# Splitting the first load of a decode attention kernel, and issuing it ahead of the branch into the block

## The chip, the core and the metric

The kernel runs on one core of one Trainium2 chip. The core has five engines with instruction streams of their own: TensorE (PE), VectorE (DVE), ScalarE (ACT), GpSimd (POOL) and SyncE (SP), which wait for each other on semaphores. Data come from HBM over 16 DMA engines, into an on-chip memory of 128 rows (partitions). The metric is the device time in microseconds; lower is better.

## The reference

One query position (Sq = 1) of 32 heads attends to 65,536 keys; four query heads share one of 8 key/value heads. All is bf16, D = 128. K and V have 134 MB each.

```python
B, Hq, Hkv, Sq, Sk, D = 1, 32, 8, 1, 65536, 128
k = jnp.repeat(k, rep, axis=1)          # rep = Hq // Hkv = 4
v = jnp.repeat(v, rep, axis=1)
scores = jnp.einsum("bhqd,bhkd->bhqk", q, k) * D ** -0.5
p = softmax(scores, axis=-1)
return jnp.einsum("bhqk,bhkd->bhqd", p, v)
```

## The kernel before

The keys of one head are cut into four units of 16,384 keys, and two units make a pair. There are 16 pairs, one for each lap of TensorE's loop. A pair's K is one transfer of 128 rows by 64 KB: row p holds 256 consecutive keys, 32 KB of them for the first unit (`n = 0`) and 32 KB for the second (`n = 1`). V is laid out in the same way. The buffers are `kbuf` and `vbuf` (both units), and `bbuf`, which holds the second unit's K so that `kbuf` can be loaded again early; in most laps POOL and ACT copy it from `kbuf`, in the others it comes straight from HBM.

For each unit TensorE transposes 128 tiles of 128 keys in groups of eight (`trb`, line 135), DVE and ACT copy the groups to `ktb` (lines 207 and 205), and TensorE multiplies them with the head's four queries (`qkb`, line 144). DVE takes the maximum, POOL reduces it over the rows, ACT makes the exponentials (`pts`, line 347), and TensorE multiplies those with V (`pvb`, line 162). After its last unit a head's sum is divided, and the result goes out at the end of the program.

All K and V transfers are issued by SP in program order (`sync_engine`, lines 398 to 448). K of lap p waits for `kfree` and V for `vfree`, which say that the buffer has been read. Lap 0 waits for nothing: its K comes in four pieces of 2 MB (`K_PIECES`, lines 26 and 407: two for `kbuf`, two for `bbuf`, each 128 rows by 16 KB), and then V as one transfer (line 437). Each piece has its own semaphore; `kp[0][0]`, here also called kp0_0, belongs to the first, and line 130 takes 16 from it ahead of a lap's first transposes. The last lap's V comes in pieces that get smaller (73, 38, 13 and 4 tiles, `V_PIECES`), so that the last piece to land is short. The 32 output rows are stored by SP at the end (lines 445 and 448).

In front of the loop DVE makes an identity matrix (`ident`), TensorE runs `PE_LEAD` small products whose result is not used (line 184), waits for the queries (`q_sem`), and transposes them. ACT issues the queries' load (line 372). Every engine enters its function by a branch into the block (lines 450 to 455), behind a barrier that all engines pass at the start of the program.

Of the kernel before, what the change touches and what calls it, by code (L numbers as in the profile page):

```python
# [10 lines left out]
P = 128  # L11
T = 128
# [4 lines left out]
LAG = 3  # L17


PE_LEAD = 48  # L20
CB = 16
HU = 4
Q = 32


K_PIECES = ((64, 64), (64, 64))
# [15 lines left out]
def starts(sizes):  # L42
    return [sum(sizes[:i]) for i in range(len(sizes))]
# [8 lines left out]
def bass_standalone__gqa_softmax__decode_kernel(nc, q, k, v, out):  # L52
    _, Hq, _, D = q.shape
# [4 lines left out]
    NP = NU // 2  # L58
    assert HR == Q and all(sum(x) == HR - R for x in OUT_ROWS) and D == P and Sk == P * T * HU and T * R == 512 and H >= 3 and HU == 4
    scale = float(D) ** -0.5  # L60
    kf, vf, qf, of = k[0], v[0], q[0, :, 0, :], out[0, :, 0, :]
# [4 lines left out]
    def sb(name, shape, dt):  # L66
        return S(nc.sbuf_tensor(name, shape, dt))

    def sem(name):
        return S(nc.semaphore(name))  # L70

    kbuf = sb("kbuf", [P, 2 * T * D], DT.bfloat16)
# [4 lines left out]
    qsb = sb("qsb", [HR, D], DT.bfloat16)  # L77
# [4 lines left out]
    identf = sb("identf", [P, P], DT.float32)  # L82
    ramp = sb("ramp", [P, Q], DT.float32)
    rampT = sb("rampT", [P, Q], DT.float32)
    cmax = sb("cmax", [P, R], DT.float32)
# [22 lines left out]
    kp = [[sem(f"kp{i}_{p}") for p in range(len(K_PIECES[i]))] for i in range(2)]  # L108
# [7 lines left out]
    cm, cma, ng, dmr, exd, sx, lrd, lra = (sem(n) for n in ("cm", "cma", "ng", "dmr", "exd", "sx", "lrd", "lra"))  # L116
    acr, l_sem, lws = sem("acr"), sem("l_sem"), sem("lws")
    xd, xa, xg = sem("xd"), sem("xa"), sem("xg")
    q_sem, o_sem, s_x, t_if, t_id, t_o, t_f, t_row = (
        sem(n) for n in ("q_sem", "o_sem", "s_x", "t_if", "t_id", "t_o", "t_f", "t_row"))  # L120

    def own(e, ins, s):
        ins.then_inc(s, 1)
        take(e, s)
# [43 lines left out]
    def pe_pair(pe, lap):  # L168
        pend = []
        for n in range(2):  # L170
            for j in range(G):
                pe_transposes(pe, n, j)
                pend.append((n, j))
                if len(pend) > LAG:
                    pe_scores(pe, *pend.pop(0))
        while pend:
            pe_scores(pe, *pend.pop(0))
        for n in range(2):
            pe_values(pe, n, lap)

    def tensor_engine(pe):
        pe.wait_ge(t_id, 1)
        for _ in range(PE_LEAD):
            pe.matmul(pvb[0][0:R, 0:R], lhsT=ident[:, 0:R], rhs=ident[:, 0:R], start=True, stop=True)
        pe.wait_ge(q_sem, 16)
        pe.transpose(qps[:, 0:HR], qsb[:, :], ident[0:HR, 0:HR]).then_inc(s_x, 1)
        pe.wait_ge(t_if, 1)
        with pe.Fori(0, NP) as lap:
            pe_pair(pe, lap)
        pe.wait_ge(t_f, H)  # L190
        pe.transpose(trb[0][0:R, 0:P], oT[:, HR - R:HR], ident[:, :]).then_inc(s_x, 1)  # L191
# [121 lines left out]
    def make_identity(e):  # L313
# [5 lines left out]
        w = 4  # L319
        while w < Q:  # L320
            own(e, e.tensor_scalar(ramp[:, w:2 * w], ramp[:, 0:w], float(w), None, ALU.add), xd)
            w *= 2
        own(e, e.transpose(rampT[:, :], ramp[:, :]), xd)
        for b in range(0, P, Q):
            ins = e.tensor_tensor(ident[b:b + Q, b:b + Q], ramp[b:b + Q, :], rampT[b:b + Q, :], ALU.is_equal)
        ins.then_inc(t_id, 1)
# [26 lines left out]
    def act_pair(e, lap):  # L353

        def copy(o, i):
            return e.activation(o, i, AF.Copy)  # L356

        for j in (3, 7, 11, 15):
            evict(e, 0, j)
            if j in ACT_COPIES:  # L360
                copy_unit(e, (lap - (WHOLE[0] - 1)) * (WHOLE[1] - lap) > 0, ACT_COPIES[j], copy, cpa, xa)
                if j == max(ACT_COPIES):
                    e.sem_inc(kfree, 1)
        for j in (3, 7):
            evict(e, 1, j)
        exps(e, 0)
        for j in (11, 15):
            evict(e, 1, j)
        exps(e, 1)

    def scalar_engine(e):
        e.dma_start(qsb[:, :], qf).then_inc(q_sem, 16)
        e.wait_ge(t_id, 1)
        e.activation(dscr[:, 0:1], ident[:, 0:1], AF.Exp, scale=1.0)
        e.activation(identf[:, :], ident[:, :], AF.Copy).then_inc(t_if, 1)
        with e.Fori(0, NP) as lap:
            act_pair(e, lap)
# [20 lines left out]
    def sync_engine(e):  # L398
        W = T * D

        def src(x, p):
            h, c = p // 2, p % 2
            return x[h, c * 2 * P * T:(c + 1) * 2 * P * T, :].rearrange("(p t) d -> p (t d)", p=P)

        def pieces(to, s, sizes, sems):
            for a, w, sm in zip(starts(sizes), sizes, sems):
                e.dma_start(to[:, a * D:(a + w) * D], s[:, a * D:(a + w) * D]).then_inc(sm, 16)

        def tokens(sems):
            for sm in sems:  # L410
                e.sem_inc(sm, 16)

        for p in range(NP):
            ks, vs = src(kf, p), src(vf, p)
            if p:
                e.wait_ge(kfree, 3 * p)
            if WHOLE[0] <= p < WHOLE[1]:
                e.dma_start(kbuf[:, :], ks).then_inc(kp[0][0], 16)
                tokens(kp[0][1:])
            else:  # L420
                for n in range(2):
                    if n and p:
                        e.wait_ge(bfree, p)
                    to, s = bbuf if n else kbuf, ks[:, n * W:(n + 1) * W]
                    if p == 0 or (p == NP - 1 and n == 0):
                        pieces(to, s, K_PIECES[n], kp[n])
                    else:
                        e.dma_start(to[:, 0:W], s).then_inc(kp[n][0], 16)
                        tokens(kp[n][1:])
                e.sem_inc(cpg, len(POOL_COPIES))  # L430
                e.sem_inc(cpa, len(sum(ACT_COPIES.values(), ())))
            if p:
                e.wait_ge(vfree, p)
            if WHOLE[0] <= p < WHOLE[1]:
                tokens(kp[1])
            if p < NP - 1:
                e.dma_start(vbuf[:, :], vs).then_inc(vp[0][0], 16)
                tokens(vp[1])
            else:
                for n in range(2):  # L440
                    pieces(vbuf[:, n * W:(n + 1) * W], vs[:, n * W:(n + 1) * W], V_PIECES[n], vp[n])
        e.wait_ge(t_o, H)
        for b, rows in enumerate(OUT_ROWS):
            for r, n in zip(starts(rows), rows):
                e.dma_start(of[r:r + n, b * Q:(b + 1) * Q],
                            orow[b * Q + r:b * Q + r + n, :]).then_inc(o_sem, 16)
        e.wait_ge(t_row, 1)
        e.dma_start(of[HR - R:HR, :], lrow[:, :]).then_inc(l_sem, 16)

    with nc.Block() as block:  # L450
        block.tensor(tensor_engine)
        block.vector(vector_engine)
        block.scalar(scalar_engine)
        block.gpsimd(gpsimd_engine)
        block.sync(sync_engine)
# [30 lines left out]
```

## Time and profile before

| What | Value |
|---|---|
| Median of 3 runs | 628.12 us (628.09 to 628.2) |
| Span of the profiled execution, first to last instruction | 626.9 us |
| Median less that span | 1.2 us |
| Read from HBM | 268.44 MB, 428 GB/s over the span |
| TensorE busy | 484.6 us (77%) |
| VectorE busy | 315.1 us (50%) |
| ScalarE busy | 228.9 us (37%) |
| GpSimd busy | 159.9 us (26%) |
| First K transfer issued | 0.72 us |
| First transposes of K | 8.18 us |

The times in the profile are counted from the first instruction's start. The span is the profiled execution's own time; the median is of other executions and includes what lies around the instructions. A line such as `L407 SPq DMA_DIRECT2D` is the time in which SP issues a transfer, not the transfer itself. In the stretches (a row begins with its start and end) the columns are the length, the busy time of TensorE's products, its weight loads, DVE, ACT and POOL with the number of instructions, TensorE's granted clock, the share of the 16 DMA engines, and GB/s; a transfer's bytes and time are counted in the stretch in which they start, so that a short stretch can show a share over 1.

### The profile page before, as it was taken

How to read it: one execution, taken by the hardware profiler on the slowest of the kernel's cores; microseconds unless marked ns; L12 is line 12 of the kernel's file. 1: busy time of each engine (PE TensorE's matmuls, PEld its weight loads, DVE VectorE, ACT ScalarE, POOL GpSimd, SP SyncE). 2: the span in 40 equal slices, each digit the busy share in tenths (PEclk: the TensorE clock that was granted, in tenths of full speed). 3: DMA queues.
4: the chain of work that ended last, by engine and by line, in shares of the span. 5: the costliest groups of instructions: out<-in, count | busy, mean ns of one | idle time of the engine just before them, and what ended most of it. 6: DMA issues, size and time to landing. Idle time of an engine off the chain costs nothing. (4 is left out here: it accounts for less than half of the span.)

```text
span 626.9 us, 27931 instructions
## 1 busy us (share of the span) xinstructions
PE 484.6 (77%) x12340; PEld 478.9 (76%) x12340; DVE 315.1 (50%) x699; ACT 228.9 (37%) x445; POOL 159.9 (26%) x124
## 2 busy tenths in 40 slices
PE   5752995959859498694976959679496894999698
PEld 5752995949859498694976959679496894999698
DVE  4620752817537174371734717356183562848274
ACT  2320532615335153341634407245062441624133
POOL 0000704307042070520605115060150702400000
PEclk9965875958769587695966959678596785969597
DMA  8999999999999999999999999999999999999997
GB/s 366 440 449 424 439 431 439 431 439 426 443 422 447 410 460 410 460 406 460 410 439 431 426 443 426 443 426 439 431 439 431 439 431 435 416 447 424 420 433 302
DMA packets 6280, 268.57 MB, mean 428 GB/s; under 512 B 896, under 2 KB 1024, under 8 KB 1152
## 3 DMA queue, kind: packets, MB, share of 16 engines
q1 hardware_dynamic: 6224, 268.45, 99.2%
q8 instruction: 6, 0.10, 0.1%
q10 hardware_dynamic: 48, 0.01, 0.0%
q14 instruction: 2, 0.02, 0.0%
HBM read 268.44 MB, written 0.01 MB: 428 GB/s over the span
## 5 line engine op out<-in xcount | busy, mean ns | idle before, releaser
L207 DVE COPY ktb<-trb 128x1024 bf16<-128x1024 bf16 x384 | 254.6, 689 | 177.5 <-PE trb L135 173.7
L205 ACT ACTIVATE ktb<-trb 128x1024 bf16<-128x1024 bf16 x128 | 131.0, 1023 | 352.7 <-PE trb L135 297.9
L135 PE MATMUL trb<-ident,kbuf 128*128 128x128 bf16 x2048 | 177.1, 245 | 104.7 <-PEq L49 104.6
L135 PEld LDWEIGHTS trb<-ident,kbuf 128*128 128x128 bf16 x2048 | 143.9, 111 | 105.6 <-issue 105.5
L213 POOL COPY bbuf<-kbuf 128x2048 bf16<-128x2048 bf16 x78 | 143.9, 1893 | 177.6 <-POOLq L49 177.6
L144 PE MATMUL qkb<-qcur,ktb 128*128 128x4 bf16 x4096 | 174.3, 165 | 11.8 <-PEq L49 10.3
L144 PEld LDWEIGHTS qkb<-qcur,ktb 128*128 128x128 bf16 x4096 | 155.2, 97 | 14.6 <-issue 14.6
L135 PE MATMUL trb<-ident,bbuf 128*128 128x128 bf16 x2048 | 157.0, 220 | 5.2 <-issue 3.9
L162 PE MATMUL pvb<-pts,vbuf 128*128 128x4 bf16 x4096 | 113.0, 166 | 15.2 <-PEq L49 11.0
L162 PEld LDWEIGHTS pvb<-pts,vbuf 128*128 128x128 bf16 x4096 | 111.1, 103 | 16.6 <-issue 15.6
L135 PEld LDWEIGHTS trb<-ident,bbuf 128*128 128x128 bf16 x2048 | 117.4, 97 | 5.5 <-issue 5.5
L393 POOL PARTITION_ALL_REDUCE cmaxa<-cmax x32 | 11.9, 370 | 254.1 <-POOLq L49 254.1
L347 ACT ACTIVATE pts<-qkb,negm 128x128 bf16<-128x128 f32 x128 | 50.9, 549 | 37.2 <-ACTq L49 37.2
L356 ACT ACTIVATE bbuf<-kbuf 128x2048 bf16<-128x2048 bf16 x26 | 49.5, 1902 | 0.0
L347 ACT ACTIVATION_READ_ACCUMULATOR pts<-qkb,negm 128x1 f32 x128 | 35.6, 278 | 0.0
L225 DVE TENSOR_REDUCE cmax<-qkb 128x4 f32<-128x512 f32 x32 | 22.0, 686 | 23.4 <-DVEq L49 23.4
L259 DVE TENSOR_TENSOR acc<-acc,pvb 128x4 f32<-128x4 f32 x16 | 2.5, 158 | 30.0 <-PE pvb L162 30.0
L257 DVE COPY acc<-pvb 128x4 f32<-128x4 f32 x8 | 1.3, 163 | 21.8 <-PE pvb L162 21.8
L395 POOL PARTITION_ALL_REDUCE la<-lp x8 | 3.4, 430 | 30.7 <-POOLq L49 30.7
L236 DVE SCALAR_TENSOR_TENSOR negm<-cmaxa,m 128x4 f32<-128x4 f32 x24 | 3.9, 163 | 11.7 <-DVEq L49 11.5
L351 ACT ACTIVATE alpha<-dm 128x4 f32<-128x4 f32 x32 | 7.1, 221 | 0.0
L250 DVE TENSOR_TENSOR acc<-acc,alpha 128x4 f32<-128x4 f32 x24 | 3.9, 164 | 6.1 <-DVEq L49 5.7
(44 smaller groups left out, 41.6 us busy)
## 6 DMA issues: line engine op xcount, KB each, us to landing
kbuf<-in_k_dram SPq DMA_DIRECT2D x4, 2048.0 KB, 16.3
bbuf<-in_k_dram SPq DMA_DIRECT2D x2, 4096.0 KB, 20.9
bbuf<-in_k_dram SPq DMA_DIRECT2D x2, 2048.0 KB, 19.9
kbuf<-in_k_dram SPq DMA_DIRECT2D x1, 4096.0 KB, 16.3
vbuf<-in_v_dram SPq DMA_DIRECT2D x1, 4096.0 KB, 21.9
vbuf<-in_v_dram SPq DMA_DIRECT2D x1, 2336.0 KB, 27.1
vbuf<-in_v_dram SPq DMA_DIRECT2D x1, 1216.0 KB, 29.6
vbuf<-in_v_dram SPq DMA_DIRECT2D x1, 416.0 KB, 30.1
```

The lines of the kernel that those rows point to most:

```text
L135: ins = pe.transpose(trb[j % NTB][:, i * P:(i + 1) * P], kv[:, t, :], ident[:, :])
L144: ins = pe.matmul(qkb[n][:, t * R:(t + 1) * R], lhsT=ktb[:, off:off + P], rhs=qcur[:, :], start=True, stop=True)
L162: ins = pe.matmul(pvb[n][:, 0:R], lhsT=vv[:, t, :], rhs=pts[n][:, t * R:(t + 1) * R], start=t == 0, stop=t == T - 1)
L205: e.activation(dst, trb[j % NTB][:, :], AF.Copy).then_inc(eva, 1)
L207: e.tensor_copy(dst, trb[j % NTB][:, :]).then_inc(evd, 1)
L213: ins = op(bbuf[:, c * CB * D:(c + 1) * CB * D], kbuf[:, off:off + CB * D])
L225: e.tensor_reduce(cmax[:, :], qkb[n][:, :].rearrange("p (t g) -> p g t", g=R), AX.X, ALU.max).then_inc(cm, 1)
L236: return e.scalar_tensor_tensor(to[:, :], cmaxa[:, :], -scale, mo[:, :], ALU.mult, ALU.min)
L347: ins = e.activation(pv[:, g, :], sv[:, g, :], AF.Exp, bias=negm[:, g:g + 1], scale=scale, accum_out=rsum[:, g:g + 1])
L351: e.activation(alpha[:, :], dm[:, :], AF.Exp, scale=1.0).then_inc(sx, 1)
L356: return e.activation(o, i, AF.Copy)
L393: e.partition_all_reduce(cmaxa[:, :], cmax[:, :], P, bass.bass_isa.ReduceOp.max).then_inc(cma, 1)
```

## The change

The first of lap 0's four K pieces is cut by rows. A load of its rows 0 to 15 (16 rows by 16 KB, `FIRST = 16`) is issued by SP from the main program, ahead of the branch into the block, on a new semaphore `kf0`. The other 112 rows follow as the first transfer in the block, on the semaphore that the whole piece had. ACT's load of the queries is moved ahead of the branch in the same way. TensorE waits for `kf0` once, ahead of its loop, and runs 47 warm-up products instead of 48. The other three K pieces and V of lap 0, and every later lap, are issued as before.

```diff
-PE_LEAD = 48
+PE_LEAD = 47
...
+FIRST = 16
...
+    kf0 = sem("kf0")
...
         pe.wait_ge(t_if, 1)
+        pe.wait_ge(kf0, 16)
         with pe.Fori(0, NP) as lap:
             pe_pair(pe, lap)
...
     def scalar_engine(e):
-        e.dma_start(qsb[:, :], qf).then_inc(q_sem, 16)
         e.wait_ge(t_id, 1)
...
-                    if p == 0 or (p == NP - 1 and n == 0):
+                    if p == 0 and n == 0:
+                        w = K_PIECES[0][0] * D
+                        e.dma_start(to[FIRST:P, 0:w], s[FIRST:P, 0:w]).then_inc(kp[0][0], 16)
+                        pieces(to[:, w:W], s[:, w:W], K_PIECES[0][1:], kp[0][1:])
+                    elif p == 0 or (p == NP - 1 and n == 0):
                         pieces(to, s, K_PIECES[n], kp[n])
...
+    w = K_PIECES[0][0] * D
+    nc.sync.dma_start(kbuf[0:FIRST, 0:w],
+                      kf[0, 0:2 * P * T, :].rearrange("(p t) d -> p (t d)", p=P)[0:FIRST, 0:w]).then_inc(kf0, 16)
+    nc.scalar.dma_start(qsb[:, :], qf).then_inc(q_sem, 16)
     with nc.Block() as block:
```

SP's instructions at the start of the program, before the change (a name in brackets is what the row waits for; sizes are rows by elements):

```order
L455 UNCONDITIONAL_BRANCH [waits barrier_Pool_Activation_PE_DVE_SP_release]
L407 DMA kbuf<-in_k_dram 128x8192 x2
L407 DMA bbuf<-in_k_dram 128x8192 x2
L437 DMA vbuf<-in_v_dram 128x32768
L418 DMA kbuf<-in_k_dram 128x32768 [waits kfree]
```

The same place on SP with the change:

```order
L457 DMA kbuf<-in_k_dram 16x8192 [waits barrier_Pool_Activation_PE_DVE_SP_release]
L465 UNCONDITIONAL_BRANCH
L429 DMA kbuf<-in_k_dram 112x8192
L409 DMA kbuf<-in_k_dram 128x8192
L409 DMA bbuf<-in_k_dram 128x8192 x2
L443 DMA vbuf<-in_v_dram 128x32768
L420 DMA kbuf<-in_k_dram 128x32768 [waits kfree]
```

The first transfer now stands between the barrier and the branch, and SP has one transfer more ahead of V and of the next lap's K. On TensorE, the start of its program with the change:

```order
L461 UNCONDITIONAL_BRANCH [waits barrier_Pool_Activation_PE_DVE_SP_release]
L186 MATMUL pvb<-ident 4x4 [waits t_id]
L186 MATMUL pvb<-ident 4x4 x46
L188 MATMUL pvb<-ident,qsb 128x32 [waits q_sem]
L191 UNCONDITIONAL_BRANCH [waits kf0,t_if]
L137 MATMUL trb<-ident,kbuf 128x128 [waits kp0_0]
```

The branch into the loop now waits for `kf0` beside `t_if`, and the first transposes for kp0_0 as before; there is one product fewer ahead of them (46 instead of 47 behind the first).

## The prediction

> **What bounds the kernel now.** I read the page's shares and slices first, then the chain that ended last, then the DMA issues, then stretches of one lap, of the end and of the start.
>
> ```profile
> PE 484.6 (77%) x12340; PEld 478.9 (76%) x12340; DVE 315.1 (50%) x699; ACT 228.9 (37%) x445; POOL 159.9 (26%) x124
> ...
> DMA  8999999999999999999999999999999999999997
> GB/s 366 440 449 424 439 431 439 431 439 426 443 422 447 410 460 410 460 406 460 410 439 431 426 443 426 443 426 439 431 439 431 439 431 435 416 447 424 420 433 302
> ...
> q1 hardware_dynamic: 6224, 268.45, 99.2%
> ```
>
> No compute engine is above 77%, while the 16 DMA engines are full in every slice but the first and the last, and SP's queue (q1) holds 99.2% of their time. One lap of the loop, as the stretches give it:
>
> ```profile
> 58.70:97.40 38.70, 29.93 (x768) 29.49 (x768) 19.88 (x45) 14.88 (x28) 12.24 (x9) 0.76 1.00 434
> ```
>
> A DMA share of 1.00 at 434 GB/s, beside 29.93 us of TensorE work in 38.7 us. So 434/16 = 27.1 GB/s for one engine, and one 16 KB row of a first-lap K piece (64 tiles of 128 bf16 columns, 16,384 bytes) takes 16,384/27.1e3 = 0.605 us. Is the queue ever empty? The DMA issues say no:
>
> ```profile
> vbuf<-in_v_dram SPq DMA_DIRECT2D x15, 26.8
> kbuf<-in_k_dram SPq DMA_DIRECT2D x13, 25.9
> vbuf<-in_v_dram SPq DMA_DIRECT2D x1, 128.0 KB, 29.9
> ```
>
> 8.39 MB (128 rows of 64 KB) at 434 GB/s need 19.3 us, yet land 25.9 or 26.8 us after their issue: each is queued behind some 6.5 us of other bytes. SP issues that far ahead, and a transfer that starts late does not catch up, because no engine idles between. How the end hangs on this, from the V tile in the last stretch, the chain in order of time, and the stretches of the end:
>
> ```profile
> L407 SPq DMA_DIRECT2D vbuf<-in_v_dram x5: 327/426/434, 592.8 to 594.6; - x5
> ```
>
> ```profile
> 620.88 2.08 PE pvb L162 x73
> ...
> 623.39 1.59 PE pvb L162 x55
> 624.98 0.02 issue
> 625.00 0.17 DVE oT L305
> 625.18 0.04 issue
> 625.22 0.28 PE trb L191
> 625.50 0.02 issue
> 625.52 0.21 DVE lrow L339
> ```
>
> ```profile
> 621.00:622.40 1.40, 1.40 (x58) 1.40 (x57) 0.49 (x3) 0.00 (x0) 0.00 (x0) 0.50 0.99 391
> 622.40:623.00 0.60, 0.60 (x23) 0.60 (x20) 0.00 (x0) 0.00 (x0) 0.43 (x1) 0.50 0.51 185
> 623.00:624.00 1.00, 1.00 (x26) 1.00 (x27) 0.18 (x1) 0.00 (x0) 0.00 (x0) 0.50 0.39 134
> ```
>
> The last V piece (128 KB) is issued at 594.6 and lands 29.9 us later, at 624.5; TensorE's last V products end at 624.98, and the tail to 626.9 is fixed. The DMA share falls from 0.99 to 0.51 at 622.4 and stays near 0.39 to 624: about half the engines are done some 1.5 us ahead of the rest. Each engine has its fixed sixteenth of every load, so **the slowest engine sets the end**, and what the start takes from it is not given back.
>
> **The change part by part.** The start now, from the timeline, the barrier's line, and the DMA shares of the first stretches:
>
> ```profile
> 0.72 0.88 SPq L407 DMA_DIRECT2D kbuf<-in_k_dram  x2
> 0.72 0.42 ACTq L372 DMA_DIRECT2D qsb<-in_q_dram  x1
> ...
> 2.94 0.33 SPq L437 DMA_DIRECT2D vbuf<-in_v_dram  x1
> ...
> 5.03 0.20 PE L186 MATMUL pvb<-ident,qsb 32*128 32x32 bf16 x1 [0.43 <-DMA qsb<-in_q_dram]
> ...
> 8.18 3.57 PE L135 MATMUL trb<-ident,kbuf 128*128 128x128 bf16 x32 [2.94 <-PEq L49]
> ...
> 19.68 0.33 SPq L418 DMA_DIRECT2D kbuf<-in_k_dram  x1
> ```
>
> ```profile
> L471 SPq EVENT_SEMAPHORE  x1: 17/17/17, 0.6 to 0.6; - x1
> ```
>
> ```profile
> 1.50:2.00 0.50, 0.00 (x0) 0.00 (x0) 0.28 (x2) 0.50 (x1) 0.00 (x0) 1.00 1.86 393
> 2.00:2.50 0.50, 0.00 (x0) 0.00 (x0) 0.28 (x2) 0.45 (x1) 0.00 (x0) 1.00 0.47 131
> 2.50:3.00 0.50, 0.00 (x0) 0.00 (x0) 0.47 (x3) 0.00 (x0) 0.00 (x0) 1.00 0.09 34
> 3.00:3.50 0.50, 0.24 (x10) 0.24 (x11) 0.28 (x4) 0.26 (x2) 0.00 (x0) 1.00 1.21 499
> ```
>
> *Earlier issue.* SP leaves the barrier at 0.6 and issues at 0.72, so the branch cannot be worth more than 0.1 us. Bytes are counted where their row starts: 393 x 0.5 = 197 KB, twelve rows, start by 2.0, and four more by 2.5 (131 x 0.5 = 66 KB). The engines' first rows are thus spread over up to half a microsecond while 128 rows are handed out; with one row for each engine that spread can shrink, by 0.5 us at most. Together 0 to -0.6 us; I take -0.25, a little under the middle, since the slowest engine need not be the one that was served last. The issue also cannot be worth less than nothing: it only moves forward.
>
> *The 16-row load.* In the trace every large load has 128 rows, eight for each engine. Here all 16 engines write at once into 16 neighbouring rows, 0 to 15. If the way into the memory belongs to the rows, as it may where 8 rows and one engine make 27.1 GB/s, then these 262 KB go through between two such groups of eight (if neighbours lie together) and all sixteen (if they are dealt out). Sixteen: 0.60 us, no loss. Two: 262/54.2 = 4.8 us, a loss of 4.2 us on every engine. No row decides between them; I take the middle in ratio of 2 and 16, rounded to four groups: 262/108.4 = 2.4 us, a loss of 1.8 us.
>
> [...]
>
> *The 112-row load.* 112/16 = 7 rows for each engine, 7 x 0.605 = 4.2 us of its time. Its rows are no longer the eight that belong together, so engines meet in one group, each at half rate. Nothing: 0. Always two together: +4.2 us. The groups are together asked for no more than before, so meetings are the smaller part: a third, +1.4 us on the engine that comes off worst. Behind it come loads of 128 rows, in which each engine is alone with its eight again: no further loss, no recovery.
>
> *The rest, at nothing.* From the K tile's rows and the warm-up's row:
>
> ```profile
> L407 SPq DMA_DIRECT2D kbuf<-in_k_dram x2: 403/412/421, 0.7 to 1.2; - x2
> ```
>
> ```profile
> 3.26 1.34 PE L184 MATMUL pvb<-ident 128*4 128x4 bf16 x48 [3.26 <-DVE ident L325]
> ```
>
> One more K issue costs SP 0.41 us, and pushes the issues of the second K piece, both pieces for bbuf and V behind it by as much; the second K piece's turn comes 8 x 0.605 = 4.8 us after the data begin, which covers it. It does not cover the 112-row load for sure: that is issued 0.41 us plus a branch behind the first, and has 0.60 us of data (2.4 with sharing) to hide behind; uncovered it would cost 0.1 us. One warm-up product less is 1.34/48 = 0.03 us, hidden under the 0.43 us that TensorE waits for the queries. The queries' load moves up by at most the same 0.1 us; its user ends at 5.23, far ahead of the first transposes at 8.18. The new wait on kf0 stands in front of TensorE's loop; nothing but that loop is behind it, and DVE and ACT wait for its transposes already. The 16 rows lie ahead of the 112 on every engine, so it adds nothing to the wait for kp0_0. The transposes then start about 3 us later, and the next K load with them (19.68 to about 22.7); the V load that it queues behind lasts far longer:
>
> ```profile
> DMA to landing us min/median/max: 28.0/34.3/40.6
> ```
>
> V of the first lap is issued at 2.94 and the two V loads of this stretch land 28.0 and 40.6 us after their issues, so it lasts to 30.9 at the least, and K has over 8 us to spare.
>
> **Sum.** -0.25 + 1.8 + 1.4 = +2.95 us. The profiled span of 626.9 becomes 629.9. The 1.2 us between that span and the median of 628.12 lie outside the instructions and stay: **631.1 us**, +0.5%.
>
> **The rivals.**
> *Rows have no shared way in (not slower).* The limit would be the engine's own 27.1 GB/s, which explains the steady stretches as well: with one engine on eight rows the two cannot be told apart. Then only the first term is left, 628.12 - 0.25 = 627.9 us. It breaks even with before where the 16 rows move at about 300 GB/s (262/300 = 0.87 us, a loss of 0.27). Chance 0.18.
> *The start covers it.* The first rows begin at 1.5 to 2.5 and the next only after 3.0: they take over 1 us instead of 0.6 already, and a slower write may hide in that. Then 1.8 - 0.7 of the second term and little of the third: 628.5 to 629.6 us, about 629. Chance 0.10.
> *The 112 rows are dealt one by one*, so that the 16 engines are always on 16 neighbouring rows: all eight rows of an engine cost 1.8 us more, 14.5 us, 642.6; half of that if the engines drift apart, 635.4. Against it: consecutive rows for an engine are the plainer dealing. Chance 0.10.
> *The change does nothing at its branch* is not a case of its own: its price of at most 0.1 us is inside every case.
>
> **How the numbers follow.** The forecast's mechanism has 0.62. Its own ends are 628.12 + 1.8 - 0.25 = 629.7 (no meetings in the 112 rows) and 628.12 + 1.8 + 4.2 = 634.1. The range goes down to the first rival with a little more of the gain, 627.7, and up to 634.1; it leaves out the third rival and the far end of the second term. A measurement of this kernel tells about 0.2%, 1.26 us, from no change: slower than 629.38 are the forecast, the third rival and some of the second, 0.62 + 0.10 + 0.04 = 0.76; within it 0.22; a gain above 1.26 us would need most of the time between the issue at 0.72 and the first steady rows after 3.0, chance 0.02.
>
> **What would show it.** Right: between 1.5 and 5 us the new profile moves visibly fewer GB/s than the 393, 131, 34 and 499 above, TensorE's first transposes begin near 11, every later lap still takes 38.7 us at a share of 1.00, and the end has a longer stretch at partial share. Wrong: the first K data land by 8.2 as now (no shared way), or a lap elsewhere is longer, which nothing here foresees. If the first transposes begin after 15, the rows are dealt one by one.

## The result: 3.7 us slower

The changed kernel takes 631.83 us (median of 5 runs, 631.55 to 632.0) against 628.12 us. The ratio is 1.0058, with a 95% interval of 1.0046 to 1.007. The profiled span went from 626.9 to 630.7 us. All medians in this text are of fast executions; two slow ones, of 657.03 us (the 14 KB control further down) and of 1116.02 us (the kernel before), are left out.

The page after the change, with its shares and slices, has the same compute and the same queue, and differs in the first slice (267 GB/s instead of 366):

```profile
span 630.7 us, 27931 instructions
...
PE 484.4 (77%) x12339; PEld 478.4 (76%) x12339; DVE 315.2 (50%) x699; ACT 228.9 (36%) x445; POOL 159.9 (25%) x124
...
DMA  9999999999999999999999999999999999999997
GB/s 267 459 410 443 424 441 436 428 445 420 449 416 457 407 461 403 461 416 449 428 433 432 432 432 432 432 436 428 436 428 436 428 441 428 422 430 449 412 432 312
```

The DMA engines count as busy for nine tenths of the first slice or more, and yet they move a quarter less: here the busy share does not tell how much data move. A stretch of one lap's length, and the end, in stretches (start and end, length, busy times, clock, DMA share, GB/s):

```profile
62.40:101.10 38.70, 29.48 (x768) 29.07 (x768) 19.88 (x45) 14.88 (x28) 12.24 (x9) 0.81 1.00 434
625.00:626.00 1.00, 1.00 (x43) 1.00 (x41) 0.47 (x3) 0.00 (x0) 0.00 (x0) 0.50 0.97 392
626.00:627.00 1.00, 1.00 (x28) 1.00 (x26) 0.18 (x1) 0.00 (x0) 0.43 (x1) 0.50 0.60 215
627.00:628.00 1.00, 1.00 (x36) 1.00 (x37) 0.00 (x0) 0.00 (x0) 0.00 (x0) 0.50 0.34 109
```

A lap still moves 434 GB/s over 38.7 us, and the end has the same shape some 3.7 us later. The loss lies in the first 12 us, as the start's timeline shows:

```profile
0.72 0.42 ACTq L459 DMA_DIRECT2D qsb<-in_q_dram  x1
...
0.72 0.39 SPq L457 DMA_DIRECT2D kbuf<-in_k_dram  x1
...
1.17 0.41 SPq L429 DMA_DIRECT2D kbuf<-in_k_dram  x1
...
5.57 0.20 PE L188 MATMUL pvb<-ident,qsb 32*128 32x32 bf16 x1 [0.99 <-DMA qsb<-in_q_dram]
...
12.03 3.18 PE L137 MATMUL trb<-ident,kbuf 128*128 128x128 bf16 x29 [6.25 <-PEq L50]
```

SP issues its first load at 0.72, exactly when it did before: nothing was gained by standing ahead of the branch. TensorE's first transposes begin at 12.03 instead of 8.18. From the stretches of the start, after the change and then before it:

```profile
2.00:4.00 2.00, 0.74 (x30) 0.74 (x31) 1.02 (x7) 0.85 (x3) 0.00 (x0) 1.00 1.14 184
4.00:6.00 2.00, 0.78 (x25) 0.57 (x20) 0.17 (x1) 0.00 (x0) 0.00 (x0) 1.00 0.71 180
6.00:8.00 2.00, 0.00 (x0) 0.00 (x0) 0.42 (x3) 0.00 (x0) 0.00 (x0) 1.00 1.18 344
8.00:10.00 2.00, 0.00 (x0) 0.00 (x0) 0.00 (x0) 0.00 (x0) 0.00 (x0) 1.00 1.00 254
```

```profile
2.00:4.00 2.00, 0.74 (x30) 0.74 (x31) 1.02 (x7) 0.86 (x3) 0.00 (x0) 1.00 0.76 299
4.00:6.00 2.00, 0.80 (x26) 0.60 (x21) 0.44 (x4) 0.00 (x0) 0.00 (x0) 1.00 0.92 393
6.00:8.00 2.00, 0.00 (x0) 0.00 (x0) 0.15 (x1) 0.00 (x0) 0.00 (x0) 1.00 1.00 426
8.00:10.00 2.00, 1.82 (x18) 1.85 (x19) 0.69 (x1) 0.00 (x0) 0.00 (x0) 1.00 1.09 467
```

Before, the stream runs at over 390 GB/s from 4 us on; after, it stays between 180 and 344 until 10 us, through the 112-row load too.

The trace also keeps the start and the time of every DMA packet, which these views do not print. A row of 16 KB takes 0.61 us in the steady stream. Over all packets of 16 KB in the first 30 us, the time above 0.605 us each (16 KB at 27.1 GB/s), shared out over 16 engines, is 0.9 us before and 4.6 us after. The difference of 3.7 us is the whole loss.

### The profile page after: what moved, and what is told of

The parts are those of the page before. It is cut to its first block, busy times and chain, and to the rows that moved or that the text cites. A ratio compares the mean times of both kernels' runs of the same rounds, so it can differ in the third digit from the quotient of the medians.

```text
span 630.7 us, 27931 instructions
## 1 busy us (share of the span) xinstructions
PE 484.4 (77%) x12339; PEld 478.4 (76%) x12339; DVE 315.2 (50%) x699; ACT 228.9 (36%) x445; POOL 159.9 (25%) x124
## 3 DMA queue, kind: packets, MB, share of 16 engines
q1 hardware_dynamic: 6240, 268.45, 99.2%
## 6 DMA issues: line engine op xcount, KB each, us to landing
vbuf<-in_v_dram SPq DMA_DIRECT2D x1, 2336.0 KB, 27.1
kbuf<-in_k_dram SPq DMA_DIRECT2D x1, 1792.0 KB, 10.7
```

## Which part of the change costs: four kernels

Theory, an assumption that the prediction made and that no view shows: a load that does not have 128 rows is slow because its rows share ways into the memory. The rivals put the loss on the place of issue, on the additional load and wait, or on very small loads alone.

**The place of issue alone.** The whole first piece is loaded ahead of the branch:

```diff
-    nc.sync.dma_start(kbuf[0:FIRST, 0:w], ...[0:FIRST, 0:w]).then_inc(kf0, 16)
+    nc.sync.dma_start(kbuf[:, 0:w], ...[:, 0:w]).then_inc(kp[0][0], 16)
     ...
-                        e.dma_start(to[FIRST:P, 0:w], s[FIRST:P, 0:w]).then_inc(kp[0][0], 16)
```

> Only one part of the change: the whole first K piece (128 rows) and the queries' load are issued ahead of the branch, no split by rows. Theory (the loss is made by loads that do not have 128 rows): no loss, within 0.2 us of the kernel before, 627.9 to 628.3 us, and SP's first issue at 0.72 as in both traces. Rival (the loads ahead of the branch make the loss): about 631.8 us.

628.27 us against 628.18 (ratio 1.0003, 0.9994 to 1.0012). Its start in the timeline:

```profile
0.72 0.40 SPq L454 DMA_DIRECT2D kbuf<-in_k_dram  x1
1.18 0.42 SPq L407 DMA_DIRECT2D kbuf<-in_k_dram  x1
```

Neither gain nor loss is seen, within an interval of -0.4 to +0.8 us, and SP issues at 0.72 with the branch in front of the load or without it.

**The split alone.** Both loads in the block:

```diff
+                        e.dma_start(to[0:FIRST, 0:w], s[0:FIRST, 0:w]).then_inc(kf0, 16)
                         e.dma_start(to[FIRST:P, 0:w], s[FIRST:P, 0:w]).then_inc(kp[0][0], 16)
     ...
-    nc.sync.dma_start(kbuf[0:FIRST, 0:w], ...)
-    nc.scalar.dma_start(qsb[:, :], qf).then_inc(q_sem, 16)   # back in ACT's function
```

> The other part alone: 16 and 112 rows, but both loads and the queries' load are issued in the block. Theory: as with the whole change, 631.5 to 632.1 us, transposes from about 12.0. Rival (the place of issue makes the loss): about 628.1 us.

631.81 us (1.0055, 1.0041 to 1.0069): the whole loss.

**As small and as early, but cut by columns.**

```diff
-    nc.sync.dma_start(kbuf[0:FIRST, 0:w], ...[0:FIRST, 0:w]).then_inc(kf0, 16)
+    nc.sync.dma_start(kbuf[:, 0:8 * D], ...[:, 0:8 * D]).then_inc(kf0, 16)
     ...
-                        e.dma_start(to[FIRST:P, 0:w], s[FIRST:P, 0:w]).then_inc(kp[0][0], 16)
+                        e.dma_start(to[:, 8 * D:w], s[:, 8 * D:w]).then_inc(kp[0][0], 16)
```

> The first load is as small (262 KB) and as early as in the change, and there are as many loads, but it is cut by columns: 128 rows by 2 KB first, then 128 rows by 14 KB. Theory (rows): no loss, 627.9 to 628.4 us. Rival (one more load, a small first load, or the second wait makes the loss): 630 to 632 us.

628.31 us (1.0004, 0.9995 to 1.0013). The DMA issues, with KB and the time to landing, of this kernel and then of the changed one:

```profile
kbuf<-in_k_dram SPq DMA_DIRECT2D x1, 1792.0 KB, 7.1
kbuf<-in_k_dram SPq DMA_DIRECT2D x1, 256.0 KB, 2.9
```

```profile
kbuf<-in_k_dram SPq DMA_DIRECT2D x1, 1792.0 KB, 10.7
kbuf<-in_k_dram SPq DMA_DIRECT2D x1, 256.0 KB, 4.5
```

The same bytes in the same number of loads land after 2.9 and 7.1 us with 128 rows each, and after 4.5 and 10.7 us with 16 and 112 rows. The additional load and the wait on `kf0` cost nothing that is seen.

**Two halves of 64 rows.** `FIRST = 64` in the changed kernel, nothing else.

> The change with FIRST = 64. Theory with groups of rows: 64 neighbouring rows reach eight of 16 groups, so each half of the piece (1.05 MB) takes 4.8 us instead of 2.4 unless the two overlap: +2.4 (one half's price, where the engines that finish early begin on the other half's groups) to +4.8 us, 630.5 to 632.9 us. Rival (only very small or unevenly dealt loads cost): 64 rows are four for each engine, 628.1 us.

633.42 us (1.0083, 1.007 to 1.0097), 5.2 us more than before. In its stretches, the time of the two halves and then the stream behind them:

```profile
4.00:12.00 8.00, 0.72 (x25) 0.58 (x21) 0.60 (x4) 0.00 (x0) 0.00 (x0) 1.00 0.99 209
14.00:20.00 6.00, 6.00 (x89) 6.00 (x87) 3.54 (x6) 1.02 (x1) 0.00 (x0) 1.00 1.01 429
```

209 GB/s, half of the 429 behind it, at a DMA share of 0.99: together the halves take twice the time of their bytes, and each two microseconds of this stretch have 197 to 221 GB/s, so nothing of an overlap shows. By the packet records, 113 of the 119 rows that start between 3 and 12 us take 1.05 to 1.35 us instead of 0.61. These loads are not very small, and 64 rows can be dealt evenly to 16 engines, four to each; so neither smallness nor a row count that does not divide explains them. The sum came out above my upper end of 4.8 us; where the other 0.4 us lie stays open.

## The price of each load by itself

Here the kernel before gets one more load behind its first two K pieces, in the steady stream, into a buffer `scr` that nothing reads. Only the rows differ; the 14 runs of the kernel before beside them had a median of 628.22 us (eleven at 628.07 to 628.33, three at 629.35 to 629.61).

```diff
                         pieces(to, s, K_PIECES[n], kp[n])
+                        if p == 0 and n == 0:
+                            e.dma_start(scr[0:16, 0:64 * D], s[0:16, 0:64 * D]).then_inc(ex, 16)
```

**Rows 0 to 15.**

> The kernel before, and behind its first two K pieces one more load: rows 0 to 15 by 16 KB (262 KB) into a buffer that nothing reads. The price of a 16-row load in the steady stream. Theory (four groups of rows): 2.4 us of all engines, 630.5 us. Rival (no shared way): 0.6 us, 628.7 us.

630.66 us, 2.44 us more (1.0039, 1.0025 to 1.0053). 0.60 us are the bytes (262 KB at 434 GB/s): **1.84 us** are the price of the 16 rows.

**The same 16 source rows into rows 0, 8, ... 120** (`scr[0:P:8, 0:64 * D]`).

> The same extra load from the same 16 source rows, but into rows 0, 8, 16 ... 120 of the unused buffer. [...] Rival (the reading side, or any load of 16 rows): as with neighbouring rows, 630.5 us.

629.62 us, 1.40 us more (1.0019, 1.001 to 1.0029); beyond the bytes 0.80 us instead of 1.84. The slowest of its runs (630.13) lies below the fastest with neighbouring rows (630.53). The stretch that holds the load, for neighbouring rows and then for spread ones:

```profile
12.00:15.00 3.00, 3.00 (x79) 3.00 (x77) 2.04 (x4) 1.44 (x2) 0.00 (x0) 1.00 1.03 191
```

```profile
12.00:15.00 3.00, 3.00 (x74) 3.00 (x73) 1.99 (x3) 1.23 (x2) 0.00 (x0) 1.00 1.02 350
```

What is read and its size are the same; only the rows written differ (the trace does not name the engine of a packet), and the rate of the stretch nearly doubles. So for 16 rows it matters which rows are written, and the reading side is not the limit. For loads of 64 and 112 rows no run changes the written rows alone; there the same cause is argued, not shown.

**Rows 16 to 127** (`scr[16:P, 0:64 * D]`), and the control, **the same bytes as 128 rows by 14 KB** (`scr[:, 0:56 * D]`).

> The kernel before with an extra load of 112 rows (16 to 127) by 16 KB (1.84 MB) into the unused buffer. Bytes alone: 4.2 us, 632.4 us. Theory (seven rows for each engine meet in the groups, as the rows of the changed kernel's trace took about 1.0 us instead of 0.61): 2.5 us more, 634.8 us. Rival (112 rows cost only their bytes; the loss was made by the 16-row load ahead): 632.4 us.

> Control: the extra load has the same 1.84 MB, as 128 rows by 14 KB. Both theories: bytes alone, 4.2 us, 632.3 to 632.5 us.

635.75 us (1.0119, 1.0102 to 1.0136) and 632.45 us (1.0066, 1.0046 to 1.0086). Their stretch of seven microseconds, 112 rows and then the control:

```profile
13.00:20.00 7.00, 7.00 (x166) 7.00 (x164) 5.35 (x9) 2.05 (x2) 0.00 (x0) 1.00 1.00 272
```

```profile
13.00:20.00 7.00, 7.00 (x166) 7.00 (x164) 5.35 (x9) 2.05 (x2) 0.00 (x0) 1.00 1.00 425
```

Bytes alone cost 4.23 us; 112 rows cost 3.3 us more (2.5 were expected), at 272 GB/s where 128 rows have 425. TensorE's, DVE's, ACT's and POOL's instruction counts and busy times in the stretch are equal to the digit, and so is the DMA share of 1.00. By the packet records, 105 rows of 16 KB that start between 12 and 24 us take 0.85 to 1.35 us instead of 0.61, in the control 4 rows: the loss is spread over nearly all 112 rows. That engines meet in a group of rows, as the prediction has it, fits this, but no run shows it.

**What the start hides.** The prices from the stream make 1.84 + 3.3 = 5.1 us (the expectations were written with 3.2 and 5.0), and the change costs 3.7. Both loads were moved to be the program's first load, each by itself, and were then put into the stream together.

> The extra load of rows 0 to 15 again (into the unused buffer), but as the program's first load instead of behind two K pieces. The two prices from the steady stream, 1.8 us (16 rows) and 3.2 us (112 rows), make 5.0, and the change costs 3.7. Theory (the slow first rows of the start hide part of the 16-row load): 1.3 us less than in the stream, 629.2 to 629.6 us. Rival (the start hides nothing, and the two loads of the change overlap instead): 630.6 us as in the stream.

> The extra load of 112 rows as the program's first load. If the start hides only what a first row takes too long in every kernel: some 0.5 to 1.3 us less than in the stream, 634.4 to 635.3 us. If the start hides nothing: 635.7 us.

> Both extra loads in the steady stream, one behind the other as in the change: 16 rows, then 112 rows (2.10 MB in all, 4.8 to 4.9 us of bytes alone). If their prices add (1.8 + 3.2): 628.2 + 4.9 + 5.0 = 638.1 us. If the 112 rows cost less behind the 16-row load (the 0.8 us that the change lacks beside 1.3 for a first 16-row load and 3.2): about 637.3 us.

| Extra load | us more than before | ratio, interval | without its bytes | in the stream |
|---|---|---|---|---|
| 16 rows first | 1.89 (630.06 - 628.17) | 1.0031 (1.0019 to 1.0043) | 1.29 | 1.84 |
| 112 rows first | 6.60 (634.77 - 628.17) | 1.0106 (1.009 to 1.0123) | 2.37 | 3.3 |
| both, in the stream | 9.86 (638.19 - 628.33) | 1.0153 (1.0136 to 1.017) | 5.0 | 5.1 if they add |

For the bytes I took 0.60, 4.23 and their sum. In the stream the prices add, as far as intervals of about 1 us to either side can tell. At the start each load costs less, by 0.55 us for the 16 rows and 0.9 us for the 112, so the start hides a part, though less of the 16 rows than I expected. One thing that it can hide is in the packet records: in the kernel before, the first sixteen rows take 1.16 us on average, 0.55 us more than the 0.61 of rows in the stream. That fits the 16 rows; no run tests it. For the pair in the change the start hides 1.4 us; where the 0.9 us beyond 0.55 come from stays open.

None of these kernels points to one that beats the kernel before: the two whose first piece kept 128 rows in each load came out at its time.

## The prediction, point by point

*The bound and the path to the end* held: a lap at 434 GB/s, a shift at the start that goes through to the end (3.7 us in the median, and as much in the span), compute unchanged. That each engine has its fixed sixteenth of every load can be seen in the packet records of before: they fall into 16 sequences, in which a row starts 3 or 4 ns before the one ahead of it ends, and from one of the queue's 4-byte writes to the next a sequence moves eight rows (395 of 400 counts between 26.5 and 540 us). At the end the first 1 KB rows of V start at 621.86, while 9.7 KB rows, two pieces ahead, run on to 622.69: an engine that is done goes on to its own next rows. Of its signs, two did not come out as said. From 2.0 to 3.0 us the new profile moves more than before, not less (165 and 101 GB/s against 131 and 34); only the sum from 1.5 to 3.5 us falls, from 0.53 to 0.42 MB. And the end has no clearly longer stretch at partial share (0.60 and 0.34 in two microseconds, against 0.51 and 0.39 in 1.6). That fits engines which were slowed much alike, where the prediction counted the one that comes off worst.

*Earlier issue, -0.25 us*, had two parts. The branch's part is nothing: SP issues at 0.72 with the branch or without it, and the whole piece ahead of the branch runs in the time before. The other part, a shorter spread of the first rows, was not measured by itself; if it exists, it is inside the 1.29 us of a first 16-row load. The queries' load did not move up either. It was issued at 0.72 again, and their transpose began at 5.57 instead of 5.03, because the load landed 4.8 us after its issue instead of 4.3; that stays off the path, as said.

*The 16-row load, +1.8 us*, is right as a price in the stream (1.84) and was too large at its place, where 1.29 was measured. Its four groups were an estimate of mine, and no run shows groups as such; the runs show rates. That the size fits so well is luck as far as the sum goes: the middle in ratio of 2 and 16 is 5.7, which lies as near to eight groups as to four, and eight would have given a loss of 0.6 us. Measured, 262 KB in 2.44 us are 107 GB/s, a quarter of 434, which is what four of sixteen would give; in 1.40 us, with the rows spread, they are 187 GB/s.

*The 112-row load, +1.4 us*, was the term that was mis-sized. Its loss is not "the smaller part": 3.3 us in the stream, nearly four fifths of the bound of 4.2 that stood for always two together. In the change it is 2.4 us if the 16 rows cost 1.29 there (3.7 - 1.29); this is what is left over, not a measurement.

*The rest at nothing* held (the split by columns has the same load and wait, at 628.31). *The sum* of +2.95 stood against +3.71. Term by term the measured side is 0.25 us higher (no gain), 0.5 lower (1.29 for the 16 rows) and 1.0 higher (2.4 left for the 112 rows). That the middle one cancels a part of the others is luck.

*The rivals.* "No shared way" fell with the spread rows (1.40 us against 2.44 for the same load). "The start covers it" is true in part, 1.4 us of 5.1 in the change, and was given as a case of its own where it was a correction to each term. "Dealt one by one" would have begun the transposes after 15; they began at 12.03, against "near 11" by the forecast.

## What to carry to other kernels

In a kernel that lives on its DMA queue as this one does (the queue fills 99.2% of the 16 engines' span), load with all 128 rows and make a load small by columns: 628.31 us here, where the cut by rows took 631.8. The loads of 16, 64 and 112 rows each slowed the stream while they lasted (191, 209 and 272 GB/s in their stretches), and the time did not come back; 112 of 128 rows cost more in sum than 16 (3.3 us and 1.84). Look for it in the GB/s, not in the DMA share, which was 0.99 to 1.03 in those stretches, and price an edit by adding the bare load to the unchanged kernel, with a control of equal bytes.

## What the runs showed of the hardware that was not expected

The price of a row count adds from load to load in the stream (5.0 measured for 5.1). A gap of seven eighths of the rows (16 instead of 128, 1.84 us) costs less in sum than a gap of one eighth (112, 3.3 us): the larger load has seven times the bytes, and at 272 GB/s it is still far from the 425 of 128 rows. And a branch between a barrier and the first load is invisible here: SP issues at 0.72 us with it and without.
